# Two groups of small matmuls put beside each other, and the steps of an attention unit spaced anew, in a kernel that weaves linear attention into an expert layer

## Chip, core and metric

The program runs on one core of one Trainium2 chip. The metric is device time in microseconds (us); lower is better. The engines are named as the profile names them: PE (TensorE, matmul; PEld is its loading of stationary operands), DVE (VectorE), ACT (ScalarE), POOL (GpSimd) and SP (SyncE, which here only issues DMAs). Each engine works through its own list of instructions in order and waits where an operand isn't ready.

## What is computed

A gated linear attention over 4 batches, 8 heads, 768 positions and 48 dimensions per head, and then 4 experts on its output, of which every expert sees all 3072 rows:

```python
# attention: q, k, v, alpha are (4, 8, 768, 48), float32
state = zeros((B, H, D, D))
for t in range(S):
    state = alpha[:, :, t, :, None] * state + einsum('bhd,bhe->bhde', k[:, :, t], v[:, :, t])
    y[:, :, t] = einsum('bhd,bhde->bhe', q[:, :, t], state)
x = y.transpose(0, 2, 1, 3).reshape(3072, 384)
# experts: w1 is (4, 384, 1024), w2 is (4, 1024, 384)
p = domain_probs / (domain_probs.sum(-1, keepdims=True) + 1e-09)
out = sum(p[:, e:e+1] * (maximum(x @ w1[e], 0) @ w2[e]) for e in range(4))
```

## The kernel before

**Units and groups.** Attention is cut into 24 units, one for each batch and each block of 128 positions, in the order of the blocks. A unit's rows of x (128 x 384) are its result. The units form groups of 2, 4, 4, 4, 4, 4 and 2; the expert layer runs over a group at a time, and while it works on one group the units of the next are computed in between.

**The expert layer.** For each group `gi` and expert `e` (a task) there is an `up` phase of 8 steps (`up`, one for each 128 hidden columns) and a `down` phase (`down`). From group 1 on an up step is 6 matmuls into `one` and 3 into `two`, with x in three parts; from group 2 on the down phase is three parts as well: for two slots of 128 rows at a time, 48 matmuls into four PSUM tiles `ops`. An up step of that kind leaves this work behind it, in this order: ACT copies `one` to `t` (L551), DVE adds `two` (L553); in the next step ACT makes `hT` (L578), DVE makes its second part (L580) and half of its third (L590). The other halves of the third part are made in the down phase that follows, one after every fourth matmul. `one`, `two` and `ops` share four PSUM buffers, so an `up` step waits for the copy and the add of two steps before, and a down phase waits until its PSUM tiles have been added to `acc` by DVE (L658; for expert 0 by ACT, L656).

**A unit's 17 steps.** `attention(u)` is a generator; each `yield` ends a step, numbered here from 0:

- 0, 1, 2: alpha, keys and queries are turned (PE `tp`, L266); alpha and keys are copied by ACT, the queries are multiplied by DVE. Each issues one DMA on SP that loads the next unit's alpha, keys or queries. Step 1 also makes the products of the diagonal on DVE (L285, L286).
- 3, 4, 5: levels 0, 1, 2 of a doubling over positions. A level is `copy_q` (two ACT copies into a block `qb`, L308), `next_q` (DVE, L315 and L317) and `next_k` (an ACT copy, L326, and a DVE product, L327). `next_q` overwrites what `copy_q` reads, and the `copy_q` of the next level reads what `next_q` wrote.
- 6: `copy_q(3)`, and the diagonal into `near` (L360).
- 7: the **first scores**: `products` of levels 0 to 3 (64 matmul records with 64 stationary columns, PE `sc`, L334), `next_q(3)`, `next_k(3)`, and two `take` (DVE, L344), which pick scores from PSUM into `near`.
- 8: `copy_q(4)`, `next_q(4)`, `next_k(4)` and two `take`. 9: `copy_q(5)`, `next_q(5)`, `next_k(5)`. 10: `copy_q(6)`, `next_q(6)`.
- 11: the **last scores**: PE `far` (L389, needs the block of `copy_q(6)`) and `products` of levels 4 and 5, both with 64 stationary columns; two `take` and `next_k(6)`.
- 12, 13: ACT copies into `lat` (L402, L406). 14: `turn_keys`, the last keys turned (PE `tp`) and copied by ACT (L452).
- 15: the **result** (PE `yps`, L428, 32 stationary columns), copied by ACT (L444).
- 16: the **state update** (PE `sps`, L463; DVE L471, L472), which reads the last `dec` of the unit, and three DMAs on SP that load the values of the unit after the next. Units of the last block have no work in step 14, and in step 16 no update.

Units 0 and 1 are placed by hand at the start; the rest by a plan.

**The plan.** `deal` gives each of these steps a time on a clock that counts the expert layer alone: an up step of four slots counts 2.1, a down slot 4.1 or 5.4. For each group it finds when its result is needed (`wanted`, less `MARGIN`, 6.0), divides the stretch since the group before by the number of units (`space`), lets unit after unit end at such distances, and has each unit begin two such spaces before its end, but not before the unit two ahead of it has ended. Within a unit step j falls due at the fraction `BEATS[j]` of the way. `advance` moves the clock, after each up step and before each down matmul, and issues whatever steps have come due there. So an attention step is always a lump of work at one place in every engine's list. At the same time the unit ahead goes first.

Of the kernel before, what the change touches and what calls it, by code (L numbers as in the profile page):

```python
# [10 lines left out]
F32 = mybir.dt.float32  # L11
# [9 lines left out]
def kernel(  # L21
# [37 lines left out]
    nc = tc.nc  # L59

    B, H, S, D = q.shape
    E, DM, F = moe_w1.shape
    P = 128
    NCB = S // P
    NP = H // 2
    HD = 64
# [15 lines left out]
    j = np.arange(P)[:, None] % HALF  # L82
# [8 lines left out]
    work = ctx.enter_context(tc.tile_pool(name="work", bufs=2))  # L91
    hid = ctx.enter_context(tc.tile_pool(name="hid", bufs=2))
    ps = ctx.enter_context(tc.tile_pool(name="ps", bufs=2, space=bass.MemoryType.PSUM))
# [37 lines left out]
    def raw(u, nm):  # L131
        return values[u % 2] if nm == "v" else apart[nm] if u == 1 else early[nm]
# [11 lines left out]
    accs = {}  # L144


    BEATS = [*(0.055 * (j + 1) for j in range(11)), 0.69, 0.75, 0.8, 0.87, 0.94, 1.0]
    MARGIN = 6.0
    waiting = deque()
    clock = 0.0  # L150
# [109 lines left out]
    def halves(t, m):  # L260
        return t.rearrange("p a (b two r) -> p a b two r", two=2, r=m)
# [7 lines left out]
    def attention(u):  # L269
        cb, b = units[u]  # L270
        ra, rk, rq, rv = (raw(u, nm) for nm in ("a", "k", "q", "v"))
# [39 lines left out]
        def next_q(li):  # L311
            m = LEVELS[li]
            qv = halves(QT, m)[:, :, :, 1, :]
            dv = halved(decs[li])
            nc.vector.tensor_mul(qv, qv, spread(dv[:, :, :, 0], m))  # L315
            dec = work.tile([P, NP, P // (2 * m)], F32, name=f"dec{li}", bufs=1)
            nc.vector.tensor_mul(dec, dv[:, :, :, 0], dv[:, :, :, 1])  # L317
            decs.append(dec)

# [33 lines left out]
        for li in range(3):  # L353
            copy_q(li)
            next_q(li)
            next_k(li)
            yield
# [6 lines left out]
        for li in range(4):  # L364
            products(li, banks[li // 2][:, li % 2])
        next_q(3)
        next_k(3)
        take(0, banks[0][:, 0])
        take(1, banks[0][:, 1])
        yield  # L370
        copy_q(4)
        next_q(4)
        next_k(4)
        take(2, banks[1][:, 0])
# [12 lines left out]
        for r in range(NP // 2):  # L387
            for s in range(2):
                nc.tensor.matmul(far[HALF * s:HALF * (s + 1), r],  # L389
                                 lhsT=KTs[6][:, 2 * r + s, :HALF], rhs=qbs[6][:, 2 * r + s],  # L390
                                 start=True, stop=True)
# [8 lines left out]
        for s in range(2):  # L400
            rows = slice(HALF * s, HALF * (s + 1))
            nc.scalar.copy(out=parts[:HALF, :, s, :, HALF:], in_=far[rows])  # L402
        yield
        for s in range(2):
            rows = slice(HALF * s, HALF * (s + 1))
# [4 lines left out]
        st = sts[b]  # L410
# [47 lines left out]

        if cb < NCB - 1:
            KB = AT  # L460
            sps = ps.tile([P, NP, 2, D], F32, name="sps", tag="w")
            for p in range(NP):
                nc.tensor.matmul(sps[:, p], lhsT=KB[:, p, :], rhs=rv[:, 2 * p:2 * p + 2, :D],  # L463
                                 start=True, stop=True)
            for i in range(2):
                rows = slice(HD * i, HD * (i + 1))
                old, add = st[rows, :, i, :], sps[rows, :, i, :]
                if cb == 0:
                    nc.vector.tensor_copy(out=old, in_=add)
                else:  # L470
                    nc.vector.tensor_mul(old, old, decs[-1][rows].broadcast_to([HD, NP, D]))  # L471
                    nc.vector.tensor_add(old, old, add)  # L472
# [197 lines left out]
    def cost(layer, gi, e):  # L670
        n = len(groups[gi]) / 4
        if layer == 0:
            return 2.1 * n if split1(gi, e) else 2.6 * n
        return 4.1 if split2(gi, e) else 5.4

    def deal():

        wanted = [0.0]  # L680
        ends = [0.0, 0.0]
        events = []
        t = 0.0
        for (gi, e), after in zip(tasks, tasks[1:]):
            part = 1 - 1 / len(groups[0]) if gi == e == 0 else 1
            t += cost(0, gi, e) * FCH * part
            if after[1] == 0:
                wanted.append(t)
            t += cost(1, gi, e) * len(groups[gi]) * part

        for gis in [*([gi] for gi in range(1, LAST - 1)), [LAST - 1, LAST]]:
            gi, due = gis[0], wanted[gis[-1]] - MARGIN
            n = sum(len(groups[i]) for i in gis)
            first = wanted[gi - 1] if gi > 1 else 0.0
            space = (due - first) / (n if gi > 1 else (n + 1) / 2)
            if gi == 1:
                space /= 2
            for k in range(n):
                u = sum(map(len, groups[:gi])) + k
                end = due - (n - 1 - k) * space  # L700
                begin = max(end - 2 * space, ends[-2])
                ends.append(end)
                run = attention(u)
                events += [(begin + (end - begin) * beat, u, run) for beat in BEATS]
        return sorted(events, key=lambda x: x[:2])

    def advance(spent):
# [5 lines left out]
    with tc.manual_schedule():  # L713
# [23 lines left out]
        def fill(n):  # L737
            for _ in range(n):
                nc.tensor.matmul(idle, lhsT=zeros, rhs=zeros, start=True, stop=True)

        runs = [attention(u) for u in range(len(groups[0]))]
        fill(8)
        for u, n in ((0, 3), (0, 6), (0, 4), (0, 5), (0, 5), (0, 4), (0, 3), (1, 0), (0, 0), (0, 2),
# [14 lines left out]
        clock = 0.0  # L758
        waiting.extend((1.0 + k, 1, runs[1]) for k in range(2))
        waiting.extend(deal())  # L760

        for (gi, e), after in zip(tasks, [*tasks[1:], (None, None)]):
# [45 lines left out]
```

## Time and profile before

Three runs took 1073.32, 1074.40 and 1075.27 us; the median is 1074.4 us.

| | before |
|---|---|
| profiled execution, us | 1073.32 |
| its span, us | 1071.6 |
| PE busy (matmul), us | 1048.1 |
| PEld busy (weight load), us | 899.1 |
| DVE busy, us | 775.2 |
| ACT busy, us | 566.7 |
| granted PE clock, mean over the span | 0.998 |
| first scores `sc` and part of last, L334, records | 2304 |
| state update `sps`, L463, records (128 stationary, 96 moving columns) | 160 |

The span is the part from the first to the last instruction of the program; the rest of the execution's time lies around it. A matmul on 32-bit floats leaves two records, one on the expert layer's reduced type leaves one. Matmuls overlap and the ends in their records are modelled, so what a group of them costs PE is read from the start of its first to the start of the next group's first, not from the durations.

### The profile page before, as it was taken

What the parts mean: (1) busy time and instruction counts of PE and PEld (TensorE: products, weight loads), DVE (VectorE), ACT (ScalarE), POOL (GpSimd) and SP (SyncE); (2) the same over time, 40 slices, a digit from 0 to 9 for tenths busy, and PEclk for the clock granted to TensorE, in tenths of its full rate; (3) what the DMA queues carried; (4) which work ended last, traced back from release to release, by engine and by line L of the source; (5) the groups of instructions that cost most, each with busy time, mean ns of one, the idle gap of its engine ahead of it and who ended that gap; (6) DMA issues with size and microseconds to landing.
All of it is one profiled execution on the core that took longest, in us unless ns stands there. A gap on an engine that the chain in (4) does not pass through costs nothing.

```text
span 1071.6 us, 21614 instructions
## 1 busy us (share of the span) xinstructions
PE 1048.1 (98%) x8460; PEld 899.1 (84%) x8460; DVE 775.2 (72%) x1711; ACT 566.7 (53%) x1202; POOL 32.7 (3%) x71
## 2 busy tenths in 40 slices
PE   8899999999999999999999999999999999999998
PEld 8777777676776798898898898898889889898988
DVE  5488776656566978778877777986787866666565
ACT  5687866575656554536546445555464543323232
POOL 2010000000000100000000000000000000000000
PEclk9999999999999999999999999999999999999999
DMA  8597699687696967758759558586594543544540
GB/s 123 156 330 216 230 328 368 238 328 241 236 309 209 402 216 274 281 160 312 268 170 359 204 187 337 186 281 234 158 358 173 221 192 147 207 177 178 187 181 31
DMA packets 158838, 251.67 MB, mean 235 GB/s; under 512 B 120112, under 2 KB 135344, under 8 KB 136208
## 3 DMA queue, kind: packets, MB, share of 16 engines
q1 hardware_dynamic: 149600, 208.82, 57.1%
q0 software_dynamic: 5760, 41.29, 9.8%
q8 instruction: 67, 1.10, 0.4%
q10 hardware_dynamic: 3376, 0.17, 0.3%
q14 instruction: 35, 0.29, 0.1%
HBM read 207.79 MB, written 42.47 MB: 234 GB/s over the span
## 4 chain that ended last, share of the span: by engine, by line
PE 83%; DVE 8%; ACT 6%; issue 2%; DMA 1%; SPq 0%; DVEq 0%; ACTq 0%
PE ops L624 25%; PE one L540 21%; PE ops L628 10%; PE two L540 10%; PE sc L334 6%; PE yps L428 3%; PE tp L266 3%; PE one L532 2%; ACT qb L308 2%; PE far L389 1%; PE sps L463 1%; DVE near L344 1%; DVE t L553 1%; DVE hT L580 1%; DVE hT L590 1%
## 5 line engine op out<-in xcount | busy, mean ns | idle before, releaser
L624 PE MATMUL ops<-w,hT 128*128 128x384 f32 x1728 | 318.0, 339 | 4.4 <-DVE acc L658 4.3
L624 PEld LDWEIGHTS ops<-w,hT 128*128 128x128 f32 x1728 | 299.1, 188 | 9.9 <-DVE acc L658 5.6
L540 PE MATMUL one<-xT,w 128*128 128x512 f32 x960 | 253.8, 400 | 2.6 <-DVE xT L248 1.1
L540 PEld LDWEIGHTS one<-xT,w 128*128 128x128 f32 x960 | 176.3, 188 | 41.8 <-DVE QT L315 1.6
L551 ACT ACTIVATE t<-one 128x512 f32<-128x512 f32 (+1 forms) x192 | 106.3, 554 | 153.6 <-PE one L540 148.5
L308 ACT COPY qb<-QT 64x256 f32<-64x256 f32 x336 | 136.4, 406 | 77.0 <-DVE QT L289 44.1
L578 ACT ACTIVATE hT<-t 128x512 fp32r<-128x512 f32 (+1 forms) x160 | 94.3, 589 | 123.6 <-DVE t L553 122.9
L580 DVE SCALAR_TENSOR_TENSOR hT<-t,hT 128x512 fp32r<-128x512 f32 (+1 forms) x160 | 102.2, 638 | 55.7 <-ACT hT L578 53.6
L540 PE MATMUL two<-xT,w 128*128 128x512 f32 x480 | 136.7, 393 | 0.0
L628 PE MATMUL ops<-hT 128*128 128x384 f32 x384 | 133.4, 491 | 0.0
L553 DVE TENSOR_TENSOR t<-t,two 128x512 f32<-128x512 f32 (+1 forms) x160 | 100.8, 630 | 41.9 <-ACT t L551 21.4
L590 DVE SCALAR_TENSOR_TENSOR hT<-hT 128x256 fp32r<-128x256 f32 x288 | 111.9, 422 | 4.4
L540 PEld LDWEIGHTS two<-xT,w 128*128 128x128 f32 x480 | 90.6, 189 | 20.0
L628 PEld LDWEIGHTS ops<-hT 128*128 128x128 f32 x384 | 69.5, 190 | 40.1 <-issue 0.4
L315 DVE TENSOR_TENSOR QT<-QT,dec 128x256 f32<-128x256 f32 x144 | 60.8, 422 | 38.2 <-ACT qb L308 37.5
L344 DVE COPY_PREDICATED near<-masks,sc 128x256 f32<-128x256 uint8 x144 | 77.0, 535 | 15.5 <-PE sc L334 12.8
L334 PEld LDWEIGHTS sc<-qb,KT 128*64 128x64 f32 x2304 | 72.7, 138 | 9.7 <-issue 5.6
L334 PE MATMUL sc<-qb,KT 128*64 128x64 f32 x2304 | 77.2, 223 | 2.6 <-ACT qb L308 2.6
L658 DVE SCALAR_TENSOR_TENSOR acc<-ops,p_all,acc 128x384 f32<-128x384 f32 x82 | 49.5, 614 | 33.9 <-PE ops L624 14.5
L326 ACT COPY KT<-KT 128x256 f32<-128x256 f32 x144 | 59.9, 416 | 3.2
L327 DVE TENSOR_TENSOR KT<-KT,dec 128x256 f32<-128x256 f32 x144 | 60.3, 419 | 0.0
L558 DVE TENSOR_TENSOR hT<-t,two 128x512 f32<-128x512 f32 x32 | 22.0, 688 | 35.6 <-ACT t L551 23.0
(88 smaller groups left out, 970.7 us busy)
## 6 DMA issues: line engine op xcount, KB each, us to landing
w<-kept SPq DMA_DIRECT2D x144, 1152.0 KB
kept<-w POOLq DMA_DIRECT2D x32, 1152.0 KB, 7.4
hT<-in_moe_w_dram SPq DMA_DIRECT2D x32, 384.0 KB
w<-in_moe_w_dram SPq DMA_DIRECT2D x48, 128.0 KB
ra<-in_alpha_dram SPq DMA_DIRECT2D x23, 192.0 KB
rk<-in_k_dram SPq DMA_DIRECT2D x23, 192.0 KB
rq<-in_q_dram SPq DMA_DIRECT2D x23, 192.0 KB
out_dram<-acc POOLq DMA_DIRECT2D x18, 192.0 KB, 6.6
```

The lines of the kernel that those rows point to most:

```text
L308: nc.scalar.copy(out=qb[rows, :, i, :].rearrange("p a (b r) -> p a b r", r=m), in_=qv[rows])
L315: nc.vector.tensor_mul(qv, qv, spread(dv[:, :, :, 0], m))
L334: nc.tensor.matmul(out[HALF * s:HALF * (s + 1), 2 * p:2 * p + 2, :], lhsT=KTs[li][:, p, HALF * s:HALF * (s + 1)], rhs=qbs[li][:, p, :, QUA ...
L344: nc.vector.copy_predicated(near.rearrange("p a (b two r) -> p a b two r", two=2, r=m)[:, :, :, 1, :], mk.unsqueeze(1).broadcast_to([P, H, ...
L540: nc.tensor.matmul(out, lhsT=w[:, part, kc], rhs=x_part(gi, part, kc), start=(part == terms[0] and kc == 0), stop=(part == terms[-1] and k ...
L551: nc.scalar.activation(out=t, in_=one, func=ACT.Copy, scale=FINE)
L553: nc.vector.tensor_add(t, t, two)
L578: nc.scalar.activation(out=top, in_=x, func=ACT.Relu, scale=TRIM)
L580: nc.vector.scalar_tensor_tensor(out=low, in0=x, scalar=0.0, in1=top.bitcast(F32), op0=ALU.max, op1=ALU.subtract)
L590: nc.vector.scalar_tensor_tensor(out=dif, in0=top.bitcast(F32), scalar=1 / 4096.0, in1=low.bitcast(F32), op0=ALU.mult, op1=ALU.subtract)
L624: nc.tensor.matmul(sums[i][part // 2], lhsT=h[:, part], rhs=w, start=(fc == 0 and part != 1), stop=(fc == FCH - 1 and part != 0))
L628: nc.tensor.matmul(sums[i][0], lhsT=h[:, 2].bitcast(F32), rhs=w, start=(fc == 0), stop=(fc == FCH - 1))
```

## The change

Four edits. `BEATS` has new fractions: steps 0 to 7 at 0.045 each (to 0.36), then 0.395, 0.43, 0.465, 0.5 for steps 8 to 11, and 0.58, 0.66, 0.76, 0.86, 1.0 for 12 to 16. `TOGETHER` names two pairs: step 15 of the unit ahead with step 7 of this one, and step 16 of the unit ahead with step 11. Where the two are nearer than a sixth of a space, `deal` gives this unit's step the very time of the other and spaces the steps between such marks in proportion. The stretch of a group begins `MARGIN` earlier, at the time at which the last unit of the group ahead ends. The state update is made in two halves of 64 stationary columns, each head on its own, into a PSUM tile of half the size; its DVE operations read the halves there. The last `dec` (level 6) gets a second buffer.

```diff
-    BEATS = [*(0.055 * (j + 1) for j in range(11)), 0.69, 0.75, 0.8, 0.87, 0.94, 1.0]
+    BEATS = [*(0.045 * (j + 1) for j in range(8)), 0.395, 0.43, 0.465, 0.5, 0.58, 0.66, 0.76, 0.86, 1.0]
+    TOGETHER = ((15, 7), (16, 11))
...
-            dec = work.tile([P, NP, P // (2 * m)], F32, name=f"dec{li}", bufs=1)
+            dec = work.tile([P, NP, P // (2 * m)], F32, name=f"dec{li}", bufs=1 + (li == 6))
...
-            sps = ps.tile([P, NP, 2, D], F32, name="sps", tag="w")
+            sps = ps.tile([P, NP, D], F32, name="sps", tag="w")
             for p in range(NP):
-                nc.tensor.matmul(sps[:, p], lhsT=KB[:, p, :], rhs=rv[:, 2 * p:2 * p + 2, :D],
-                                 start=True, stop=True)
+                for i in range(2):
+                    rows = slice(HD * i, HD * (i + 1))
+                    nc.tensor.matmul(sps[rows, p, :], lhsT=KB[:, p, rows], rhs=rv[:, 2 * p + i, :D],
+                                     start=True, stop=True)
             for i in range(2):
                 rows = slice(HD * i, HD * (i + 1))
-                old, add = st[rows, :, i, :], sps[rows, :, i, :]
+                old, add = st[rows, :, i, :], sps[rows]
...
-            first = wanted[gi - 1] if gi > 1 else 0.0
+            first = wanted[gi - 1] - MARGIN if gi > 1 else 0.0
...
-                events += [(begin + (end - begin) * beat, u, run) for beat in BEATS]
+                due_at = {-1: begin, **{j: begin + (end - begin) * BEATS[j] for j in (7, 11, 16)}}
+                for ahead, j in TOGETHER:
+                    if times and abs(times[-1][ahead] - due_at[j]) < space / 6:
+                        due_at[j] = times[-1][ahead]
+
+                beats = [0.0, *BEATS]
+                marks = sorted(due_at)
+                times.append([])
+                for lo, hi in zip(marks, marks[1:]):
+                    times[-1] += [due_at[hi] if j == hi else
+                                  due_at[lo] + (due_at[hi] - due_at[lo]) * (beats[j + 1] - beats[lo + 1])
+                                  / (beats[hi + 1] - beats[lo + 1]) for j in range(lo + 1, hi + 1)]
+                events += [(time, u, run) for time in times[-1]]
```

More of the change, by code (lines that the diff above doesn't have):

```diff
@@ L682, in deal @@
         events = []
+        times = []
         t = 0.0
```

## The prediction

> **What bounds the kernel now.** I read the page first. PE is busy nearly all the time and most of the chain that ended last is PE's; by stages of the span, PE was busy 339.9 of the 340.0 us between 235 and 575 us. So what a lump of attention costs PE is paid in full there, and a wait of PE elsewhere is paid too.
>
> ```profile
> PE 1048.1 (98%) x8460; PEld 899.1 (84%) x8460; DVE 775.2 (72%) x1711; ACT 566.7 (53%) x1202; POOL 32.7 (3%) x71
> PE 83%; DVE 8%; ACT 6%; issue 2%; DMA 1%; SPq 0%; DVEq 0%; ACTq 0%
> ```
>
> Then PE's own timeline around one unit (start, duration, what). The result and the first scores already stand in one lump; the state update stands alone; the last scores stand 13 us later.
>
> ```profile
> 402.21 0.85 PE L540 MATMUL two<-xT,w 128*128 128x512 f32 x3
> ...
> 404.65 2.09 PE L334 MATMUL sc<-qb,KT 128*64 128x64 f32 x64
> 406.67 1.67 PE L540 MATMUL one<-xT,w 128*128 128x512 f32 x6
> 408.18 0.85 PE L540 MATMUL two<-xT,w 128*128 128x512 f32 x3
> 408.86 1.54 PE L540 MATMUL one<-xT,w 128*128 128x512 f32 x6
> 410.24 0.85 PE L540 MATMUL two<-xT,w 128*128 128x512 f32 x3
> 410.92 1.02 PE L463 MATMUL sps<-rv,AT 128*128 128x96 f32 x8
> 411.73 1.63 PE L540 MATMUL one<-xT,w 128*128 128x512 f32 x6
> ...
> 424.32 0.66 PE L389 MATMUL far<-qb,KT 128*64 128x128 f32 x8
> 424.81 1.10 PE L334 MATMUL sc<-qb,KT 128*64 128x64 f32 x32
> ```
>
> Third, DVE's timeline in an up phase, and the two kinds of wait that PE has today:
>
> ```profile
> 566.32 0.68 DVE L553 TENSOR_TENSOR t<-t,two 128x512 f32<-128x512 f32 x1
> ...
> 568.79 0.68 DVE L553 TENSOR_TENSOR t<-t,two 128x512 f32<-128x512 f32 x1
> ```
> ```profile
> 63.72 0.69 PE L334 MATMUL sc<-qb,KT 128*64 128x64 f32 x16 [1.20 <-ACT qb L308]
> ...
> 765.17 2.35 PE L624 MATMUL ops<-w,hT 128*128 128x384 f32 x12 [1.90 <-DVE acc L658]
> ```
>
> PE does an up step in 2.06 us (408.18 to 410.24). DVE's adds follow each other at 2.47 us, because add, `hT` on ACT (0.63), second part (0.70) and half third part (0.42) form a loop. So in an up phase DVE falls back 0.4 us per step even without attention, and only a lump on PE lets it catch up. That decides what the new places cost.
>
> **State update in halves.** Today 410.92 to 411.73, 0.81 us for 8 records, with no delay on entry: 0.1 us apiece, though each streams 96 columns against the 0.17 us of an `ops` with 384; the load of 128 stationary columns sets it. Six early ones, among two-record matmuls, take 0.87 (86.13 to 87.00). Afterwards there are 16 records with 64 stationary and 48 moving columns. No row has that. Nearest is `sc`: 64 and 64 columns, (2.09 - 0.22)/63 = 29.6 ns apiece. Lower end 22 ns (48/64 of it), upper end 55 ns (`far`, 64 and 128 columns). I take 29.6: the same stationary load, nearly the same moving one. That is 0.47, and 0.05 for the joint, as between `far` and `sc`: 0.52 us. Beside the last scores the way in and out of the narrow form is paid already. Saved: 11 x 0.29 + 6 x 0.35 = 5.3 us for the 17 units in which the planner's formulas make the two coincide. Units 0, 1 and 5 stand alone: 0.09 in, 0.44, 0.15 out, 0.69 us; saves 0.4 in all. By the ends the 17 save 7.2 or lose 1.7.
>
> The Trainium skill, "TensorEngine Tiling (Array Packing)", section Instruction Overhead, speaks against the halves: about 60 cycles per matmul however few columns, and no tiling of a dimension that is small already. With the 2.4 GHz of its page "Trainium Kernel Development and Optimization", section NeuronCore Architecture, I estimate 16 x 25 ns = 0.40 us against 8 x 40 ns = 0.32 us for 96 columns, a loss of 0.08 us per unit if streaming set the pace. The row's 0.1 us apiece says that it doesn't.
>
> **Result beside first scores.** Where the two stand apart today (units 12 and 13) the steps from `two` to the next `one` take 2.45 (485.90 to 488.35) and 2.79 us (494.88 to 497.67) where 0.68 (408.18 to 408.86) is usual: 3.88 together. In one lump: 406.67 - 402.21 - 0.68 = 3.78. The step from 32 to 64 columns costs nearly as much as leaving, so a merge saves 0.1. Five neighbours are apart today, one afterwards: 0.4 us. Merging is nearly done already; this part brings little.
>
> PE saves 5.3 + 0.4 + 0.4 = **6.1 us**.
>
> **New places, late units (6 on).** An up phase and its down phase are 16.8 + 16.4 on the plan's clock, and so is the spacing now. A unit's end then falls 6.0 before the end of an up phase, and steps 7 to 11 into 9.3 of these 16.8: after up step 0 result and first scores, after 1 step 8, after 2 step 9, after 3 or 4 step 10, after 3 to 5 update and last scores. Today steps 9 to 11 lie mostly in the down phase. Queued behind them on ACT and DVE are copies, adds and `hT`, for which PE's buffers wait. From DVE's rows: step 8 is 0.42 + 0.34 + 0.9, step 9 0.76, step 10 0.42, the update 4 x 0.35, the last takes and key product 1.3. With start 0 at up step 1 and each operation put in its engine's order:
> - `copy_q(6)` ends near 11.35; PE comes to `far` at 10.35 + 0.09 + 0.47 = 10.9: a wait of 0.45 where step 10 is only one step ahead (group 3), none where it is two (0.45 for four units).
> - DVE ends the up phase 3.2 us behind, from the end of `two` to the end of its add (today up to 3.5, without a stall). In the down phase it owes the last `hT` by 5.0 us, then the diagonal product 1.1, seven third-part halves 2.5, the queries 0.69 and the add to `acc` 0.61: 9.9. PE reaches the next slots, which need that buffer, at 48 x 0.174 + 0.5 = 8.9. A wait near 1.0 for units with expert above 0; 1.8 once, where a level falls in front too.
> Summed over groups 2 to 4: 7.5 us. The same sum for today's 593.30 gives 1.2, where 0.64 was seen, so I take 5.5. Today's late waits (593.30, 677.00, 714.89, 765.17, 833.64, 851.84: starts less the usual distance) are 5.9, and their causes move away. Net 0; ends -4 and +4.
>
> **Early units (2 to 5).** Spaces are 11.5, and steps 8 to 11 lie within 2.4 of the plan, 4.5 today. From the first scores' end to the last copy the engines need takes 1.5, then 0.42 + 0.81 + 0.42 + 0.81: 4.0 us and more where a weight piece is split in between (0.85 on ACT, 0.95 on DVE). PE has until then 3.9, 1.8, 5.0 and 3.8: some 3 to 5 us of waits, 2 to 4 more as levels 0 to 3 are pressed too. Against it, waits of 1.3 (63.72, 80.25, 84.12) and 1.6 (121.38) exist today, and ACT catches up during each new one. I take +3; ends 0 and +8.
>
> **Costed at nothing.** Steps 0 to 2 issue the same three loads on SP, step 16 three (0.4 to 0.8 us each), past SP's weight pieces; a unit's raw inputs have half a unit, some 40 us, until they are read, its values more. POOL issues nothing new. If that cover went, PE's `tp` would wait for a landing. The second `dec` buffer takes away a wait: without it `next_q(6)` would overwrite what the update ahead still reads. The halved DVE operands have the same 64x192 elements.
>
> **Sum.** -6.1 + 3.0 + 0 = -3.1 us: the profiled execution's 1073.3 becomes 1070.2. It is the fastest of three and lies 1.1 under the median, so against 1074.4 the forecast is **1071.3 us**. About 0.2% (2.1 us) is what can be told from no change here.
>
> **Rivals.**
> - *Waits of the pressed levels eat it all.* `far` waits for `copy_q(6)` and the next slots for `acc`: for it the loop of 2.47 against 2.06 and the early ACT, busy 38.8 of 51 us from 29 to 80 us; against it, around 750 us today's plan has step 10 at up step 4 and last scores at step 6, lags to 3.85 us, and no wait at `far`. It turns slower when new waits exceed old ones by 6.1 + 2.1; at +6.5 early and +3 late it gives 1074.4 + 3.4 = 1077.8. Chance 0.24.
> - *The halves cost 55 ns apiece.* PE then loses 1.7 + 0.8 and gains 0.4: with +3 of waits 1079.5. For it only that `far` does; against it `sc`. 0.06.
> - *A draw*, waits some 5 or 6 more: 1074. 0.20. Update and last scores failing to meet would end here too: 0.69 alone instead of 0.81 saves 2 to 3, less 3 of waits.
>
> **Chances.** The forecast has 0.50, its own range 1067.5 (no net waits early, one less late) to 1072.2. Range for all: 1067.5 to 1077.8; what the 55 ns would give lies outside. Faster 0.50, same 0.20, slower 0.30.
>
> **What shows it.** Right: `sps` with 16 records right before `far`, some 0.5 us to `far`'s start, `yps` and `sc` adjoining in all but one pair, PE's busy time about 6 us less. Wrong: gaps before `far` released by `qb` L308 at most units, or before `ops` released by `acc` L658, summing to more than 12 us after 500 us or 60 to 130 us; or `sps` records at 50 ns.

## The result: slower by 1.1%, and the profile after

The changed kernel took 1086.56 us (median; 1083.02 to 1088.26), the kernel before 1074.84 us beside it: a ratio of 1.0106 with a 95% interval of 1.0078 to 1.0134. The forecast was 1071.3 us with a range up to 1077.8, so its direction and its range are both wrong. The profiled execution took 1086.72 us (span 1085.0, mean granted clock 0.994), 13.4 us more than the profiled one of before.

The page of after, busy time and the chain by engine:

```profile
PE 1049.7 (97%) x8620; PEld 893.1 (82%) x8620; DVE 772.1 (71%) x1711; ACT 568.6 (52%) x1202; POOL 32.7 (3%) x71
...
PE 76%; DVE 13%; ACT 7%; issue 2%; DMA 2%; SPq 0%; DVEq 0%; ACTq 0%
```

PE's busy time is no smaller, though its work is, and DVE has 13% of the chain where it had 8%: PE now waits more, and the chain behind its waits runs through DVE. Where it waits, by the view of PE's waits (total us, times, longest), first before, then after:

```profile
PE ops L624 <- DVE acc L658: 4.3, 4, 1.9
PE far L389 <- ACT qb L308: 3.1, 3, 1.6
PE yps L428 <- ACT lat L406: 3.1, 4, 1.5
PE sc L334 <- ACT qb L308: 2.6, 3, 1.2
```
```profile
PE far L391 <- ACT qb L310: 16.7, 9, 3.4
PE sc L336 <- ACT qb L310: 4.9, 7, 1.5
PE ops L628 <- DVE acc L662: 3.4, 5, 1.6
```

The wait of the last scores (`far`) for the block of `copy_q(6)` has grown by 13.6 us; the one for `acc` has not. Where in time: two stretches of the span, with the busy time of PE, PEld, DVE, ACT and POOL, the granted clock, the DMA share and GB/s, before and then after.

```profile
50.00:100.00 50.00, 45.54 (x426) 35.30 (x425) 40.95 (x90) 41.91 (x94) 3.33 (x6) 1.00 0.79 252
100.00:150.00 50.00, 48.55 (x532) 39.16 (x531) 38.36 (x85) 37.69 (x83) 3.72 (x7) 1.00 0.82 263
```
```profile
50.00:100.00 50.00, 41.16 (x405) 32.39 (x402) 35.79 (x80) 35.12 (x81) 3.34 (x6) 0.93 0.76 242
100.00:150.00 50.00, 43.74 (x461) 32.70 (x460) 35.62 (x82) 36.37 (x78) 2.65 (x5) 0.97 0.66 199
```

PE did 4.4 and 4.8 us less in each 50 us, and was granted less clock: 0.93 and 0.97 where it had 1.00. The starts of phases set side by side agree: the delay of after against before is 1.7 us at 65 us, 10.3 at 100, 15.4 at 117, and 15.55 at the first up phase of group 1 (165.38 became 180.93). Two phases later it is 15.95, and by the end 13.4. So all of the loss, and more, arises before 216 us, and nearly all of it (15.5 us at 166 us) in the stretch of units 2 to 5. From 216 us on the change gains 2.5 us.

What makes up that +15.95 can only be counted, to a microsecond or two. By the busy time of 50 us stretches PE's idle time up to 200 us grew by 10.7 us (14.6 to 25.2); by PE's starts less their usual distance the waits grew by some 12 us. Four windows of 3.41 us at half clock, each of which loses up to 1.7 us (an estimate: half its length), stand against one, some 5 more. The halved updates and the merges save about 1.4 there. The sum is 14 to 16.

One unit shows both. PE's timeline in after (start, duration, what, idle before and its releaser), and then two neighbouring stretches:

```profile
86.22 0.69 PE L336 MATMUL sc<-qb,KT 128*64 128x64 f32 x16 [1.46 <-ACT qb L310]
86.83 1.56 PE L632 MATMUL ops<-hT 128*128 128x384 f32 x4
88.32 0.67 PE L467 MATMUL sps<-rv,AT 128*64 128x48 f32 x16
92.36 1.12 PE L391 MATMUL far<-qb,KT 128*64 128x128 f32 x8 [3.37 <-ACT qb L310]
```
```profile
88.60:92.02 3.42, 0.39 (x14) 0.27 (x10) 3.15 (x10) 2.22 (x7) 0.00 (x0) 1.00 0.91 350
92.05:95.40 3.35, 3.04 (x41) 2.92 (x42) 1.28 (x5) 0.26 (x1) 0.00 (x0) 0.50 0.45 148
```

The first scores leave PE at 86.83; 2.1 us of work follow, then nothing for 3.4 us, and then the last scores run at clock 0.50: 8 records of `far` are modelled at 1.12 us where 0.66 was usual. What kept `far` is in the chain of waits of that stretch (start, duration, what):

```profile
84.94 0.60 DVE near L362
85.55 0.92 DVE w L230
...
86.49 0.96 DVE w L232
87.44 0.34 DVE QT L317
...
87.88 0.34 DVE KT L329
88.22 0.65 DVE near L346
...
88.89 0.72 DVE near L346
89.61 0.06 DVE QT L317
...
91.08 0.33 DVE QT L317
...
91.49 0.41 ACT qb L310
...
91.91 0.41 ACT qb L310
...
92.36 1.12 PE far L391 x8
```

Up to 91.5 it is DVE's list without a break, and then two copies on ACT. `copy_q(6)` needs `next_q(5)` (91.08), and in front of it in DVE's order stand a piece of weights being split (L230 and L232, 1.88 us, of which the last 0.6 lie behind the first scores' end), the four takes (L346) and two levels of `next_q` and `next_k`. From the first scores' end this took 5.5 us here. In the unit at 109 us it took 8.0: one weight split was nearly over when the scores ended (107.34 to 109.28), a second stood in the middle (112.37 to 114.30), and the last 2.4 us were ACT's, mostly copies. PE's 5.4 us of work in between left a wait of 2.6.

The parts that were forecast well can be seen at a late unit, in PE's timeline of after:

```profile
415.23 1.56 PE L544 MATMUL one<-xT,w 128*128 128x512 f32 x6
...
417.33 1.56 PE L544 MATMUL one<-xT,w 128*128 128x512 f32 x6
...
420.83 0.86 PE L544 MATMUL two<-xT,w 128*128 128x512 f32 x3
421.62 0.67 PE L467 MATMUL sps<-rv,AT 128*64 128x48 f32 x16
422.12 0.62 PE L391 MATMUL far<-qb,KT 128*64 128x128 f32 x8
422.57 1.10 PE L336 MATMUL sc<-qb,KT 128*64 128x64 f32 x32
```

The update of 16 records stands right before `far`, which starts 0.50 us later without a wait. But an up step now takes 2.10 us (415.23 to 417.33) where it took 2.06. Nothing in the change touches it; that is taken up below.

### The profile page after: what moved, and what is told of

Its sections match the earlier page's. It is cut to its first block, busy times and chain, and to the rows that moved or that the text cites. A ratio compares the mean times of both kernels' runs of the same rounds, so it can differ in the third digit from the quotient of the medians.

```text
span 1085.0 us, 21981 instructions
## 1 busy us (share of the span) xinstructions
PE 1049.7 (97%) x8620; PEld 893.1 (82%) x8620; DVE 772.1 (71%) x1711; ACT 568.6 (52%) x1202; POOL 32.7 (3%) x71
## 4 chain that ended last, share of the span: by engine, by line
PE 76%; DVE 13%; ACT 7%; issue 2%; DMA 2%; SPq 0%; DVEq 0%; ACTq 0%
PE ops L628 24%; PE one L544 20%; PE two L544 10%; PE ops L632 9%; PE sc L336 5%; PE yps L430 3%; PE tp L268 2%; ACT qb L310 2%; DVE near L346 2%; DVE t L557 2%; PE one L536 2%; DVE hT L584 2%; DVE QT L317 1%; DVE hT L594 1%; PE far L391 1%
## 5 line engine op out<-in xcount | busy, mean ns | idle before, releaser
L628 PE MATMUL ops<-w,hT 128*128 128x384 f32 x1728 | 314.8, 339 | 3.5 <-DVE acc L662 3.4
L544 PE MATMUL one<-xT,w 128*128 128x512 f32 x960 | 257.1, 402 | 1.9 <-DVE xT L250 1.8
L557 DVE TENSOR_TENSOR t<-t,two 128x512 f32<-128x512 f32 (+1 forms) x160 | 100.8, 630 | 43.4 <-PE two L544 25.2
L346 DVE COPY_PREDICATED near<-masks,sc 128x256 f32<-128x256 uint8 x144 | 77.1, 535 | 28.6 <-PE sc L336 25.7
L336 PE MATMUL sc<-qb,KT 128*64 128x64 f32 x2304 | 80.0, 226 | 4.9 <-ACT qb L310 4.9
L536 PE MATMUL one<-xT,w 128*128 128x256 f32 (+1 forms) x240 | 45.9, 340 | 0.6 <-ACT xT L446 0.6
```

The lines of the kernel that those rows point to most:

```text
L336: nc.tensor.matmul(out[HALF * s:HALF * (s + 1), 2 * p:2 * p + 2, :], lhsT=KTs[li][:, p, HALF * s:HALF * (s + 1)], rhs=qbs[li][:, p, :, QUA ...
L346: nc.vector.copy_predicated(near.rearrange("p a (b two r) -> p a b two r", two=2, r=m)[:, :, :, 1, :], mk.unsqueeze(1).broadcast_to([P, H, ...
L544: nc.tensor.matmul(out, lhsT=w[:, part, kc], rhs=x_part(gi, part, kc), start=(part == terms[0] and kc == 0), stop=(part == terms[-1] and k ...
L557: nc.vector.tensor_add(t, t, two)
L628: nc.tensor.matmul(sums[i][part // 2], lhsT=h[:, part], rhs=w, start=(fc == 0 and part != 1), stop=(fc == FCH - 1 and part != 0))
```

## The experiments

Theory A: the pressed steps of units 2 to 5 cost everything (a wait at `far`, and the clock that falls after it), and the rest of the change brings what was forecast. Rivals: B, the halves cost what they were to save; C, the late places cost; D, the second `dec` buffer shifts other tiles. Ratios are to the kernel before on the same chip, with 95% intervals.

**Early units on the old fractions.** The changed kernel, with the units of group 1 (2 to 5) placed as before.

```diff
+    EARLY = [*(0.055 * (j + 1) for j in range(11)), 0.69, 0.75, 0.8, 0.87, 0.94, 1.0]
...
+                if gi == 1:
+                    times.append([begin + (end - begin) * beat for beat in EARLY])
+                    events += [(time, u, run) for time in times[-1]]
+                    continue
```


> The changed kernel, with units 2 to 5 back on the old fractions. Theory (early): the loss arises where spaces are 11.5, because steps 8 to 11 leave the chain of copies and products of three levels no time, so PE waits at `far` and `sc`. Then the waits between 55 and 190 us fall back from about 38 to about 20 us, the clock of a half returns to one window, and the time is 1066 to 1070 us, below both kernels. Rival (late): DVE's loop in the up phases is what costs; then little comes back here, 1083 to 1086 us. Rival (halves): the update in halves costs; then 1080 us or more.

1074.88 us, ratio 1.0011 [0.9997, 1.0026]. The loss is gone and in the profile no window at half clock is left before the end (the mean granted clock of its ten executions goes from 0.997 to 1.000), but the forecast's gain doesn't appear. At group 1's first up phase it is still 2.6 us behind the kernel before. A new wait shows: 1.9 us at 136.8 us, where `tp` of unit 6 waits for its queries to land.

**The new fractions for units 2 to 5 alone.** The kernel before, with only these units on the new `BEATS`, and the second `dec` buffer.

```diff
-                events += [(begin + (end - begin) * beat, u, run) for beat in BEATS]
+                events += [(begin + (end - begin) * beat, u, run) for beat in (EARLY if gi == 1 else BEATS)]
```


> The kernel before, with units 2 to 5 alone on the new fractions (their ends as before), and the second buffer of the last `dec`. Theory (early): it takes up nearly the whole loss, 16 to 20 us, so 1090 to 1094 us, with three more windows of half the clock. Rival (late): 1074 to 1078 us.

1092.07 us, 1.0173 [1.0148, 1.0197]: alone it loses more than the whole change does. By the phase at 216 us its profile is 15.3 us behind, about as the change (15.95); after that it falls back by 4.4 more, with the slower matmuls that the second buffer brings (below) and one more window at half clock at 784 us, where the change gains. With the run before, this settles where the loss is made: taking the early fractions out removes it, putting them in alone brings it.

**The halves alone, and the change without them.** First the kernel before with the update in 64-column halves, then the changed kernel with the old update of 8 records.

```diff
-            sps = ps.tile([P, NP, 2, D], F32, name="sps", tag="w")
+            sps = ps.tile([P, NP, D], F32, name="sps", tag="w")
...
+                for i in range(2):
+                    rows = slice(HD * i, HD * (i + 1))
+                    nc.tensor.matmul(sps[rows, p, :], lhsT=KB[:, p, rows], rhs=rv[:, 2 * p + i, :D],
+                                     start=True, stop=True)
```


> The kernel before, with the state update in 64-column halves and nothing else. By the changed kernel's trace 16 records take 0.45 us and 0.15 us out, so each lump alone costs about 0.69 us where it cost 0.81 to 0.87: theory, 2 to 3.5 us faster, 1071 to 1073 us. Rival (halves cost): no change or slower, 1074 us or more.

> The changed kernel, with the state update as before (128 stationary, 96 moving columns), between the result of the unit ahead and `far`. If the halves save what the prediction worked out (0.29 to 0.35 us in 17 units), it is 5 to 6 us slower than the changed kernel: 1091 to 1093 us. If they save nothing because PE waits at `far` anyway in early units, 3 to 4 us: 1090 us. Rival (halves cost): 1080 us.

Halves alone: 1074.0, 1.0012 [1.0000, 1.0024], where 1071 to 1073 was expected: no gain that can be told. In its profile PE was 3.3 us ahead of the kernel before at 688 us, of which 1.3 came between 165 and 188 us, where only the kernel before has a window at half clock; at 777 it was 2.0 ahead. In between, a down phase waits for `acc` a little longer (2.16 us at 761.62) and a window at half clock follows, which the kernel before doesn't have there. None of the ten executions was granted the full clock (0.996 to 0.998); of the kernel before beside them 7 of 19 were:

```profile
758.10:761.50 3.40, 1.36 (x8) 1.04 (x6) 3.40 (x12) 2.83 (x7) 0.00 (x0) 1.00 0.26 105
761.55:764.90 3.35, 3.28 (x10) 3.28 (x11) 3.29 (x9) 0.00 (x0) 0.00 (x0) 0.50 0.00 0
```

Without the halves: 1090.43, 1.0153 [1.0127, 1.0179], as expected; against the change's own 1.0106 the halves are worth 0.5%, about 5 us, though the two intervals just overlap. By the timelines the wide update costs 0.35 us more in each of the 17 units (0.95 us to the start of `far` against 0.50, less 0.1 on the way in); in four of them PE waits at `far` anyway, and the other 13 give 4.6. B falls as the cause of the loss, for without the halves nothing of it comes back; that they save 5 us rests on the timelines, and no run of its own resolves it.

**Only the last levels of units 2 to 5 spread out.** The changed kernel with steps 8 to 16 of these units at later fractions; first scores as in the change.

```diff
+    EARLY = [*(0.045 * (j + 1) for j in range(8)), 0.44, 0.52, 0.6, 0.69, 0.74, 0.79, 0.83, 0.86, 1.0]
```


> The changed kernel with steps 8 to 16 of units 2 to 5 late again: last scores at 0.69 as before, first scores still at 0.36. Theory (last levels): if the pressing of steps 8 to 11 is what costs, the waits of 1.2 to 3.4 us at `far` between 69 and 140 us go, with two windows of half the clock: 1075 to 1079 us. Rival (all levels pressed, first scores as much): about half of the loss comes back, 1080 to 1083 us.

1078.06, 1.0035 [1.0024, 1.0045]. Of the 1.06% some 0.7 points go with the places of steps 8 to 16, of which the change put 8 to 11 within 0.14 of the way. The total wait of `far` for `qb` falls from 16.7 us in nine to 7.5 in five. What is left to the 1.0011 of the first run, 0.24%, is probably the pressed levels 0 to 3; no run separates it.

**PE kept busy in the gaps.** The changed kernel with matmuls that nothing reads: 22 before `far`, 12 before each of levels 2 and 3 of the first scores, units 2 to 5 only.

```diff
+        if 2 <= u < 6:
+            for _ in range(22):
+                nc.tensor.matmul(far[:HALF, 0], lhsT=ident_all[:, :HALF], rhs=ident, start=True, stop=True)
```


> The changed kernel with matmuls that serve nothing put into PE's list for units 2 to 5: 22 before `far`, 12 before each of levels 2 and 3 of the first scores; their output is overwritten. PE then works where it waited. Theory (clock): each window of 3.4 us at half the clock follows a wait and costs 1.7 us; of the four windows between 61 and 188 us two or three go, 3 to 5 us faster than the changed kernel, less up to 1.5 for fillers that outlast a wait: 1082 to 1085 us. Rival (the windows have another cause): they stay, 1086 to 1088 us.

1096.54, 1.0210 [1.0195, 1.0225], a miss: the 22 (44 records) took 4.9 us on PE, more than the gap that they were to fill, and the run is 10 us slower than the change. It does show that the half clock comes from the gaps: the windows at 61, 92 and 140 us are gone, and the only one before the end lies at 196, behind a wait for `xT` that has no filler. What the clock alone costs no run isolates. Executions of one program support the count of up to 1.7 us a window: beside the first two runs of this section the kernel before took 1072.1 us on average in the seven executions granted 1.000, and 1073.6 in the five granted 0.998, which is one window: 1.5 us.

**The takes moved a step later.** In all units the two pairs of `take` leave steps 7 and 8 for 8 and 9, so that `next_q` comes ahead of them on DVE: once on the changed kernel, once on the best version below.

```diff
         next_k(3)
-        take(0, banks[0][:, 0])
-        take(1, banks[0][:, 1])
         yield
         copy_q(4)
         next_q(4)
         next_k(4)
-        take(2, banks[1][:, 0])
-        take(3, banks[1][:, 1])
+        take(0, banks[0][:, 0])
+        take(1, banks[0][:, 1])
```


> The changed kernel with each pair of `take` one step later: those of levels 0 and 1 behind the products of step 8, those of levels 2 and 3 behind those of step 9. The work is the same; on DVE the products that `copy_q(5)` and `copy_q(6)` wait for come sooner by one pair (0.9 to 1.5 us) each. Theory (DVE's list is the chain): the waits at `far` between 69 and 176 us, 11.5 us in the changed kernel, fall by 1 to 2.4 us each, 4 to 8 us in all, and one or two windows of half the clock go: 1078 to 1083 us where the kernel before takes 1074. Rival (the copies on ACT are the chain): they stay, 1086 us.

> The same edit in the best version so far (early units on the old fractions, second group's start as before, buffer behind `hT`), 1068.1 us. There `far` waits on ACT only three times (802.87 us, 1.70, is the longest). Theory: those shrink, and the waits for `acc` stay as they are: 0.5 to 2 us faster, 1066 to 1068 us. Rival (the `take` now delay the adds that free PE's buffers): 1069 us or more.

1094.80, 1.0183 [1.0168, 1.0199], and 1081.07, 1.0058 [1.0046, 1.0071]: both misses, and slower than the version without the edit, by about 8 and 11.5 us going by the ratios. At the early units the waits of `far` shrank only from 3.37, 2.64 and 2.14 us to 3.18, 1.92 and 1.96: weight splits and levels still fill DVE's list. In the later units a step later means among the adds that PE's buffers wait for, as the rival had it. That fits PE's waits in the second of the two runs (without the edit the first is 4.1 in five, and the second isn't there), but these two lines make up 3.8 us of its loss and two windows at half clock at most 3.4; the rest was not traced:

```profile
PE ops L630 <- DVE acc L664: 5.9, 6, 2.2
...
PE two L546 <- DVE t L559: 2.0, 7, 0.5
```

**Where the tiles lie.** A second `dec` buffer of 32 bytes a partition moves what is allocated behind it, `xT` and `hT` among it. First the kernel before with that buffer and nothing else, in an unchanged order; then the changed kernel with three buffers, a shift of 64 bytes.

```diff
-            dec = work.tile([P, NP, P // (2 * m)], F32, name=f"dec{li}", bufs=1)
+            dec = work.tile([P, NP, P // (2 * m)], F32, name=f"dec{li}", bufs=1 + (li == 6))
```


> The kernel before with a second buffer of the last `dec`, which nothing needs there: the order of all work is unchanged, `xT` and what follows lie 32 bytes further. Theory (place): 512-column matmuls go to 233.4 ns, `ops` to about 177; 2 to 5 us slower, 1076 to 1079 us. Rival: no change, 1073 to 1075 us.

> The changed kernel with three buffers of the last `dec` instead of two, nothing else: x's parts (`xT`) and all that is placed behind them lie 64 bytes further than before the change, not 32. Theory (place): the second buffer moved `xT` by 32 bytes, and that is why matmuls with 512 columns follow each other at 233.4 ns in the changed kernel and at 229.3 before, 5.9 us over 1440 of them, while `ops` gained 1 to 2 ns. Then they return to 229 ns here, `ops` to 178 to 179 ns, and the time is 2 to 5 us below the changed kernel's: 1081 to 1084 us where the kernel before takes 1074. Rival (the steps' order does it): pitch stays at 233, 1086 us.

The buffer alone: 1076.17, 1.0018 [1.0009, 1.0028], about 2 us for nothing but an address. Its timeline has the up step of 2.10 us (414.79 to 416.89):

```profile
414.79 0.86 PE L540 MATMUL two<-xT,w 128*128 128x512 f32 x3
...
416.89 0.86 PE L540 MATMUL two<-xT,w 128*128 128x512 f32 x3
```

Its matmuls of 512 columns follow each other at 233.5 ns on average, against 229.4 before, over the whole span. The shift by 64 bytes was expected to restore 229 and had 232.7; that run took 1090.53, 1.0157 [1.0140, 1.0175], 4 us above the change in the timed runs and not above it in its profile (span 1084.8). The profiled execution is the fastest of its four, granted 0.996 of the clock where the other three have 0.991 to 0.993 and those of the change 0.994 to 0.998, so a part at least is the clock; why it fell lower is open.

**The second buffer behind `hT`,** so that `xT` and `hT` lie as before; in the changed kernel, and in the version with the early units on old fractions.

```diff
+            dec = (hid.tile([P, NP, P // (2 * m)], F32, name="dec6b", bufs=1) if li == 6 and u % 2 else
+                   work.tile([P, NP, P // (2 * m)], F32, name=f"dec{li}", bufs=1))
```


> The changed kernel with nothing but the second buffer moved behind `hT`. Theory (place): 512-column matmuls at 229 ns, `ops` at 178 to 179; 2 to 3 us faster than the changed kernel, 1082 to 1085 us where the kernel before takes 1074, so that the early units are left with 8 to 11 us of loss. Rival: 233 ns and 1086 to 1088 us.

> The run with units 2 to 5 on the old fractions, and the second buffer of the last `dec` put behind `hT`, so that x's parts and `hT` lie where they lay before the change. Theory (place): 512-column matmuls back at 229 ns, some 2 to 3 us faster than with the buffer in front, 1071 to 1073 us. Rival (the buffer's place doesn't matter, something else of the changed order slows them): 233 ns, 1074 to 1075 us.

The distance is 229.3 ns again in both. The times are 1085.66, 1.0119 [1.0105, 1.0134], and 1073.21, 1.0003 [0.9993, 1.0014]. In the profile the first is 2.0 us shorter than the change; the timed ratios, 1.0106 against 1.0119 and 1.0011 against 1.0003, don't resolve it.

**The second group's units later.** The last version, with the stretch of group 2 beginning where it did before the change; then with a pad that puts `hT` where the change had it and leaves `xT`.

```diff
-            first = wanted[gi - 1] - MARGIN if gi > 1 else 0.0
+            first = wanted[gi - 1] - MARGIN * (gi > 2) if gi > 1 else 0.0
```


> The same, and the stretch of the second group's units (6 to 9) beginning where it did before the change, 6.0 later. Theory: the 2.06 us that PE waits at 136.8 us for unit 6's queries, whose load was issued late on SP, go: another 1 to 2.5 us, 1069 to 1072 us, below both kernels. Rival: the wait moves to another place, no change.

> The run before the last one with 32 bytes left free between x and `hT`, so that x's parts lie as before the change and `hT` as after it. Theory (place, each tile for itself): 512-column matmuls 229 ns and `ops` some 1 to 2 ns quicker, 1 to 3 us over 1728 of them: 1067 to 1070 us. Rival (only the distance between tiles counts): one of the two pitches is as in the worse kernel, 1071 us or more.

**1068.09 us, 0.9951 [0.9938, 0.9964]: faster than both kernels.** No window at half clock is left before the last microseconds, and PE's busy time is 7.8 us less than before:

```profile
PE 1040.3 (98%) x8620; PEld 889.3 (83%) x8620; DVE 772.1 (72%) x1711; ACT 566.8 (53%) x1202; POOL 32.8 (3%) x71
```

Phase by phase it is 3.0 us behind the kernel before at 188 us, 1.4 ahead at 216 and 5.0 ahead at the end. PE's wait for `xT`, 1.8 us in the first run of this section, is 0.4; unit 6's queries still land late (a wait of 1.8 us at 137.5), so that the earlier stretch was not what made them late: the time is below the range expected, and not for the reason given. How the gain over the version before it divides is not settled further. The pad: 1068.81, 0.9960 [0.9948, 0.9973], no difference that can be told in the time; but its 512-column matmuls stay at 229.3 ns, and the `ops` on `hT` go from 174.3 to 173.4, so each of the two goes with its own tile's place.

## Why the prediction was wrong, by its own steps

**Right: the update in halves.** Forecast 0.52 us with the joint, 0.29 saved in eleven units and 0.35 in six; measured 0.50 (421.62 to 422.12), which saves 0.31 and 0.36. The two meet in all 17 units as the formulas gave. In the fastest version PE is busy 7.8 us less than before; less about 1.7 for the window at half clock of before, that is about the 6.1 forecast, though there the two meet in 14 units only. The prediction's estimate by the Trainium skill, "TensorEngine Tiling (Array Packing)", section Instruction Overhead, was 0.40 us for the 16 records, beside 0.32 for the eight if streaming set the pace. The first is near what was measured (0.45), the second is not (0.81 us with 128 stationary columns), so that the loss of 0.08 us a unit did not come, and the rows decide.

**Nearly right: result beside first scores.** Units 5 and 6 alone stay apart, as forecast. PE's rows have the two adjoining 20 times where before has 13, so seven joined and not four; at 0.1 us apiece that is 0.7 instead of 0.4, too little to be told in the time.

**Right in sum: the late units.** Net 0 was forecast, within 4 either way. PE's idle time between 200 and 900 us, by its busy time, is 6.2 us against 5.05, 1.15 more. The waits for `acc` at expert above 0 came (0.93, 0.75, 0.36, 0.37, and 1.81 once; 1.0 and 1.8 were forecast), those of 0.45 at `far` in group 3 did not. Three waits at `far` came that were not forecast: 1.8 and 1.1 us at units 6 and 7 (175 and 210 us, in the stretch that is called early here) and 1.6 at 821 us. With the one at 175 the late units cost 3.0 more: the sum holds, its items only in part. C falls as the cause of the loss.

**Wrong: the early units, "I take +3; ends 0 and +8".** Measured +15.95 by the phase that starts 216 us into the span before, with about 1.4 of the saving in it: some 17 us against the 3, or 14 without the waits of units 6 and 7. Three things in that step failed, and each pushed the same way:
- *The chain from the first scores to `far` was taken as 4.0 us*, with a weight split as "4.0 us and more" that entered no number. Measured 5.5 and 8.0: in the first unit the takes (2.1 us) and the last 0.6 of a split, in the second a whole split (1.9 us), the takes and an add to `acc` (0.6) stand in the middle of the chain, because DVE works in order.
- *A credit was given because "ACT catches up during each new" wait.* It was mostly DVE that was behind, and DVE hardly idled in these waits (busy 3.15 of the 3.42 us from 88.60): it is what the chain runs through. The waits removed (1.2, 1.5 and 1.0 us at 80, 121 and 165 us of before) were less than those made, so waits grew by 11 to 12 us in all.
- *The clock was not priced at all*, though the trace of before has a window at half clock right after a wait (0.97 granted between 150 and 200 us). Three more such windows cost some 5 us by the estimate above, a third of the loss.

**Not in the sum: the address of `xT`.** The buffer was costed at nothing; it costs about 2 us by the run that had nothing else (0.9 to 2.8 per mille). D holds as a small part there; in the changed kernel the timed runs don't resolve it.

The first rival named the right mechanism, in the right place, the wait at `far` for `copy_q(6)`, though it named ACT's load as the reason and not DVE's list. It was given 6.5 us early, less than half of what came, and a lower chance than the forecast. With what was measured the sum is 15.95 early (1.4 of the saving is in it), -4.7 for the rest of the saving, +0.1 late (1.15 less the 1.1 at 210 us, which is in the early part already) and +2 for the address: 13.4, as between the two profiles; with counts good to a microsecond or two, that it agrees so closely is luck.

## What to carry to other kernels

When steps are pressed together, follow the dependency chain through the in-order list of every engine that it crosses, with all other work that stands in that list, and compare that with the work of the waiting engine in between; a fraction of the span in which the engine "is not busy" says nothing of it. In a stretch that is already broken up, price a wait of PE at its length plus the slower clock that can follow. Before a new buffer is called free, look whether it moves an operand of the hot loop.

## What the runs showed of the hardware

**The half clock goes by a fixed grid and by PE's share of it.** Windows at half clock before the end of the program are 3.413 us long or twice that, and within a run they start at whole multiples of that length from each other (in after at 61.32, 92.04, 139.83 and 184.20 us: 9, 14 and 13 lengths apart). Fourteen traces that have such a window were cut along its grid, and the lengths that ran at full clock were sorted by PE's load: where PE's modelled busy time was below 0.43 of a length, the next length ran at half clock in 23 cases of 23; between 0.43 and 0.51 in 12 of 19; above 0.51 in none of some 4,300. So 1.7 us of waiting were enough where they fell into one length (57.90 to 61.32 us in after, busy 1.72 us of 3.42). The Trainium skill, "TensorE: Matmul & The Clock Gate", section "What's actually happening", gives the same free-running window of 3413 ns and the half rate after an idle one; these runs agree on the length and the grid, and differ in that a window need not be idle, only less than about half busy.

**An address sets the pace of a matmul.** Shifting `xT` by 32 bytes a partition (with `hT` and others) took 512-column matmuls from 229.4 to 233.4 ns apart, and those on `hT` from 174.6 to 174.0 (173.6 in the changed kernel). In the last run, with the pad, `hT` alone of the two is shifted, and only its matmuls change (229.3 and 173.4). Which places are good, and why, stays open: 64 bytes gave 232.7 and 175.9.
